# Threshold attention with a Fourier mixing block: q and k transposed by VectorE in 32x32 blocks, and one block-diagonal score product for the last 64 queries

## The chip, the core and the metric

The kernel runs on one core of a Trainium2 chip. The metric is the device time of one execution in microseconds. The engines are TensorE (PE; its weight loads are listed as PEld), VectorE (DVE), ScalarE (ACT), GpSimd (POOL) and SyncE (SP), which issues most DMAs. TensorE writes to PSUM; the other data lie in SBUF.

## The reference

Attention in 8 batches of 8 heads, 576 queries and keys, head dimension 64, all float32. A weight counts only where its score lies within tau of the row's maximum. Then a Fourier mixing over sequence and channels, and a normalised two-layer channel network with 512 and 2048 channels.

```python
scores = (1 / sqrt(64)) * q @ k.transpose(0, 1, 3, 2)      # q, k, v: (8, 8, 576, 64)
thresh = max(scores, -1) - tau
scores = where(scores >= thresh, scores, -1e9)
attn = exp(scores - max(scores)); attn = attn / (sum(attn) + 1e-9)
x = (attn @ v) with heads side by side                      # (8, 576, 512)
u = x + real(fft over channels of fft over sequence of x)
un = (u - mean(u)) / sqrt(var(u) + 1e-6)
out = u + relu(un @ w_ch1) @ w_ch2                          # float64 in memory: 512 x 2048, 2048 x 512
```

## The kernel before

The attention works on pairs of heads: 4 pairs in each of 8 batches, so 32 pairs, numbered n. A pair has 5 steps, t = 0 to 4, so there are 160 steps i = 5n + t. Steps 0 to 3 take 128 queries of each of the two heads. Step 4 takes the last 64 queries of both heads together, head j on partitions 64j to 64j+63 of one tile.

`load_pair(n)` (L124) fetches q and k of a pair with ten DMAs into `qk_in`, rows of 64 floats (256 bytes) per query or key, so that the tokens lie on the partitions. For k of the second head the blocks are placed so that its transposed columns come out rotated by 64. There is one such buffer (`bufs=1`). `prep_in_parts(n)` (L389) turns the pair round: four PE transposes into `pq` (L398), evacuated by DVE into `qT` with the factor q_scale (L399); four into `pk` (L405), evacuated by ACT into `kT` (L406); one into `pt` (L409), evacuated by DVE in two parts (L410, L413). Then it issues `load_pair(n + 1)`. In `qT` and `kT` head j lies on partitions 64j to 64j+63, the columns are tokens.

`scores(i)` (L423) multiplies: for t < 4 four products of 64 rows, two heads by two halves of 288 keys (L433); for t = 4 five products of 64 rows and 64 columns (L444), one of them cut because of the rotated columns. `softmax(i)` (L450) takes the row's maximum on DVE (L461), the exponential on ACT (L469), the threshold and sum on DVE (L477), and later scaling on DVE and ACT (L492, L496). `weights_in_parts` (L512) transposes the weights on PE (L560), `weighted_values` (L569) multiplies with v (L589). Each matmul appears as two records in the profile.

PSUM is used through two rings: "sc" with two score tiles, and "mm" with four banks that all other PE results share, the transposes among them.

Between the attention's steps lies other PE work. `mixing` does the Fourier part of the batch before, `channels` and `channels_in_quarters` do the channel network: hidden layer products (L822, L926), output products (L848, L1090). `fill()` (L1169) takes as much of it as a budget per slot allows. POOL does sums for these products (`s_w` L909, `t_u` L900, `s_tile` and `hs` L1086), and the folding of x (`half` L622, after an exchange of two rows by DMA, L607 and L609).

There are three parts. In the first batch, `step(i)` (L1185) puts all engines' instructions in order by hand and prepares the next pair at t = 4; there is no channel work yet, so `busy` issues matmuls whose result is not used, and the weights are converted from float64 on the side. In the second batch, `second_batch(i)` (L1316) is ordered by hand too and prepares at t = 3, between the second and third `fill()`. From the third batch on, the loop at L1387 fixes only the order of PE; the other engines' order is made by the framework's scheduler. There the three parts of the preparation are spread over the step t = 3. After the last attention step, what is left of the channel network runs alone.

Of the kernel before, what the change touches and what calls it, by code (L numbers as in the profile page):

```python
# [47 lines left out]
def kernel(  # L48
# [75 lines left out]
    def load_pair(n, queue=nc.sync):  # L124
        b, p = n // NPAIR, PAIRS[n % NPAIR]
        hs = [2 * p + (j + p) % 2 for j in range(2)]

        qk = sb.tile([128, 9, 2, D], FP32, tag="qk", bufs=1, name="qk_in")
        for j, h in enumerate(hs):
            nc.sync.dma_start(  # L130
                out=qk[:, 0:4, j, :], in_=q[b, h, 0:512, :].rearrange("(t p) d -> p t d", p=128)
            )
            nc.sync.dma_start(out=qk[0:64, 8, j, :], in_=q[b, h, 512:576, :])


        h = hs[0]
        queue.dma_start(
            out=qk[:, 4:8, 0, :], in_=k[b, h, 0:512, :].rearrange("(t p) d -> p t d", p=128)
        )
        queue.dma_start(out=qk[64:128, 8, 0, :], in_=k[b, h, 512:576, :])  # L140
        h = hs[1]
        queue.dma_start(out=qk[0:64, 4, 1, :], in_=k[b, h, 512:576, :])
        rows = k[b, h, 0:512, :].rearrange("(t r p) d -> p r t d", r=2, p=64)
        queue.dma_start(out=qk[64:128, 4:8, 1, :], in_=rows[:, 0])
        queue.dma_start(out=qk[0:64, 5:8, 1, :], in_=rows[:, 1, 0:3])
        queue.dma_start(out=qk[64:128, 8, 1, :], in_=rows[:, 1, 3])
        loaded[n] = qk

    def load_v(n):

# [20 lines left out]
    for u in range(2):  # L171
        for j in range(2):
            nc.gpsimd.memset(v_in[u][64 - 64 * j : 128 - 64 * j, 8 + j, :], 0.0)
    eps = const.tile([128, 1], FP32, name="eps")
    nc.vector.memset(eps[:], 1e-6)

# [205 lines left out]
    xs = {}  # L382
    sums = {}

    def prep_pair(n):
        for _ in prep_in_parts(n):
            pass

    def prep_in_parts(n):  # L389


        qk = loaded.pop(n)
        qT = sb.tile([128, S], FP32, tag="qT", name="qT")
        kT = sb.tile([128, S], FP32, tag="kT", name="kT")

        pq = ps.tile([128, 512], FP32, tag="mm", bufs=4, name="pq")
        for t in range(4):
            nc.tensor.transpose(pq[:, 128 * t : 128 * t + 128], qk[:, t, :, :], ident[:, :])  # L398
        nc.vector.tensor_scalar(  # L399
            out=qT[:, 0:512], in0=pq[:, :], scalar1=q_scale[:, :], scalar2=None, op0=ALU.mult  # L400
        )
        yield
        pk = ps.tile([128, 512], FP32, tag="mm", bufs=4, name="pk")
        for t in range(4):
            nc.tensor.transpose(pk[:, 128 * t : 128 * t + 128], qk[:, 4 + t, :, :], ident[:, :])  # L405
        nc.scalar.copy(kT[:, 0:512], pk[:, :])  # L406
        yield
        pt = ps.tile([128, 512], FP32, tag="mm", bufs=4, name="pt")
        nc.tensor.transpose(pt[:, 0:128], qk[:, 8, :, :], ident[:, :])  # L409
        nc.vector.tensor_scalar(  # L410
            out=qT[:, 512:S], in0=pt[:, 0:64], scalar1=q_scale[:, :], scalar2=None, op0=ALU.mult
        )
        nc.vector.tensor_copy(kT[:, 512:S], pt[:, 64:128])  # L413
        heads[n] = (qT, kT, v_in[n % 2])
        if n + 1 < B * NPAIR:
            load_pair(n + 1)

    def normalized(n):

# [3 lines left out]
    def scores(i):  # L423
        n, t = divmod(i, NT)
        qT, kT = heads[n][0:2]

        nh = 2 if t < 4 else 1
        sc = [ps.tile([128, 2, 512], FP32, tag="sc", name=f"sc{j}") for j in range(nh)]
        if t < 4:
            for c in range(2):  # L430
                for j in range(2):
                    hp = slice(64 * j, 64 * j + 64)
                    nc.tensor.matmul(  # L433
                        sc[j][:, c, 0:HALF], qT[hp, 128 * t : 128 * t + 128],
                        kT[hp, HALF * c : HALF * (c + 1)], start=True, stop=True,
                    )
        else:

            for j, c, c0, k0, w in (
                (0, 0, 0, 0, HALF), (1, 0, 0, 64, HALF), (0, 1, 0, HALF, HALF),  # L440
                (1, 1, 0, 64 + HALF, 512 - HALF), (1, 1, 512 - HALF, 0, 64),
            ):
                hp = slice(64 * j, 64 * j + 64)
                nc.tensor.matmul(  # L444
                    sc[0][hp, c, c0 : c0 + w], qT[hp, 512:S], kT[hp, k0 : k0 + w],
                    start=True, stop=True, skip_group_check=True,
                )
        steps[i] = (sc, nh)

# [735 lines left out]
    def step(i):  # L1185

        n, t = divmod(i, NT)
        scores(i)

        def last_stages():  # L1190
            run = chunks.pop(i - 1, None)
            for _ in range(2 if run else 0):
                next(run, None)

        if t == 1 and n > 0:
            softmax(i, lambda: weighted_values(n - 1, 1), last_stages)
            load_v(n + 1)
        elif t == 3:
            softmax(i, lambda: weighted_values(n, 0), last_stages)
        else:  # L1200
            softmax(i, None, last_stages)
        if t == 1 and n > 0:
            pass
        elif later and later[0][0] <= i:
            later.pop(0)[1](i)
        else:
            busy(2 if i < NCHUNK else 1)
        if t == NT - 1:
            prep_pair(n + 1)
        if i in chunks:  # L1210
            next(chunks[i])
        if i > 0:
            transposed_weights(i - 1)
        if i in chunks:
            next(chunks[i])
        while after and after[0][0] <= i:
            after.pop(0)[1]()
        if i > 0 and i + 3 < NCHUNK:
            chunks[i + 3] = w1_chunk(i + 3)
        if t == 2 and n > 0:  # L1220
            folds.append(fold_rows(n - 1))
        if folds and next(folds[0], True):
            folds.pop(0)
# [27 lines left out]
    raw = load_dim()  # L1251
    load_seq()
    chunks[1] = w1_chunk(1)
    prep_pair(0)
    load_v(0)
    chunks[2] = w1_chunk(2)
# [59 lines left out]
    def second_batch(i):  # L1316

        nonlocal budget
        n, t = divmod(i, NT)
        first = i - per_batch  # L1320
        if first != 1:
            scores(i)
        if first == 0:

            transposed_weights(i - 1)
        softmax(i, None, lambda: (advance(first - 1), advance(first - 1)))
        chunks.pop(first - 1, None)
        transfers(first)
        fold_more()
        if first == 0:  # L1330
            weighted_values(n - 1, 1)
            scores(i + 1)
            column_means(LAST)
            copy_mean(LAST)
            folds.append(fold_rows(n - 1))
            while folds:
                fold_more()
            load_v(n + 1)
            start_batch(0)
            mix(3)  # L1340
            mix(3)
        elif first == 1:
            mix(3)
            transposed_weights(i - 1)
            mix(2)
            mirrored(LAST)
            for c, eng in ((1, nc.vector), (3, nc.vector), (0, nc.gpsimd), (2, nc.gpsimd)):
                less_mean(eng, LAST, c)
            advance(first)
            advance(first)  # L1350
        elif first == 2:
            mix(2)
            transposed_weights(i - 1)
            mix(2)
            weighted_values(n, 0)
            advance(first)
            advance(first)
        else:
            fill()
            transposed_weights(i - 1)  # L1360
            advance(first)
            advance(first)
            fill()
            if t == 3:
                prep_pair(n + 1)
            fill()
            if t == 2:
                weighted_values(n, 0)
            if t == 0:
                weighted_values(n - 1, 1)  # L1370
                folds.append(fold_rows(n - 1))
                load_v(n + 1)
        if first == 16:
            fold_halves(1)
        if first < 3:
            budget += 3 * per_slot
# [10 lines left out]
    for i in range(2 * per_batch, total + 1):  # L1387
# [4 lines left out]
        n, t = divmod(i, NT)  # L1392
        if t > 2:
            fold_more()
        nothing = iter(())
        prep = prep_in_parts(n + 1) if t == 3 and n + 1 < B * NPAIR else nothing
        weights = weights_in_parts(i - 1)
        next(prep, None)
        fill()
        next(weights, None)  # L1400
        fill()
        next(weights, None)
        next(prep, None)
        if i < total:
            softmax(i)
        fill()
        next(prep, None)
        if t == 2:
            weighted_values(n, 0)
        if t == 0:  # L1410
# [60 lines left out]
```

## Time and profile before

| | |
|---|---|
| Time, median of 3 runs | 1670.19 us (1670.05 to 1670.26) |
| Span of the profiled execution | 1669.6 us |
| Preparations of pairs, first and last start | 9.4 us, 1409.9 us |
| First scores, last scores of t = 4 | 11.6 us, 1462.7 us |
| q1, the queue of nearly all transfers | 128854 packets, 55.35 MB |
| HBM read, written | 46.02 MB, 9.44 MB |

Times in the profile are microseconds unless marked ns. A group of instructions is given by line, engine, operation, tile written and tiles read, shape and count. A tile query gives for each line the shortest, median and longest duration in ns, then the first and last start. A list of waits gives engine and line, what was waited for, and then the total in us, the number of waits and the longest. In a list in order of time an entry has its start and its length; several equal instructions in a row are merged, and lengths of matmuls in a row overlap.

### The profile page before, as it was taken

Reading aid. Unit: us, or ns where it says so; the run is one execution under the profiler, and the core shown is the slowest. Engines: PE = TensorE matmul, PEld = TensorE weight load, DVE = VectorE, ACT = ScalarE, POOL = GpSimd, SP = SyncE. Lnnn points to the kernel's source line nnn. Section 1 sums busy time; section 2 is a strip of 40 time slices with the busy share of each in tenths; the row PEclk is TensorE's granted clock in tenths of the full one; section 3 lists DMA queues with packets and bytes.
Section 4 is the critical chain, followed back from the end, with each engine's and each line's share of the span. In section 5 each row is a group of like instructions: output and inputs, shape, how many; then the busy total and the mean of one; then the engine's idle time right before and its main releaser. Section 6 shows DMA issues by size and latency. Waiting matters only on the chain.

```text
span 1669.6 us, 28885 instructions
## 1 busy us (share of the span) xinstructions
PE 1621.8 (97%) x10826; PEld 1273.6 (76%) x10826; DVE 1146.0 (69%) x2518; ACT 837.9 (50%) x1817; POOL 581.9 (35%) x779
## 2 busy tenths in 40 slices
PE   8998899999999999999999999999999999999998
PEld 4555555577887888878888778887878788889998
DVE  6887785567757686857566858686677768664454
ACT  5775675544455454545354546454646455532111
POOL 5674562041321442134332143213242244215232
PEclk9999999999999999999999999999999999999999
DMA  5423222100010101000101010111001010000000
GB/s 157 121 55 110 73 73 56 30 20 21 19 39 15 29 15 42 23 28 8 28 22 35 10 34 15 42 22 29 22 16 42 22 32 4 14 1 13 14 13 13
DMA packets 130384, 57.48 MB, mean 34 GB/s; under 512 B 121123, under 2 KB 121125, under 8 KB 130246
## 3 DMA queue, kind: packets, MB, share of 16 engines
q1 hardware_dynamic: 128854, 55.35, 12.3%
q8 instruction: 86, 1.41, 0.4%
q14 instruction: 52, 0.43, 0.1%
q10 hardware_dynamic: 1392, 0.30, 0.1%
HBM read 46.02 MB, written 9.44 MB: 33 GB/s over the span
## 4 chain that ended last, share of the span: by engine, by line
PE 76%; DVE 15%; ACT 7%; issue 2%; POOL 1%; DVEq 0%; ACTq 0%; POOLq 0%
PE ph L926 23%; PE po L1090 18%; PE pv L589 8%; PE sc L433 7%; PE pw L560 5%; PE po L848 3%; DVE e L477 3%; DVE neg L461 2%; ACT e L469 2%; DVE hs L1051 2%; PE sc L444 2%; PE ph L822 1%; PE py L692 1%; PE pa L709 1%; PE pn L782 1%
## 5 line engine op out<-in xcount | busy, mean ns | idle before, releaser
L469 ACT ACTIVATE e<-sc,neg 128x576 f32<-128x576 f32 x288 | 212.6, 738 | 238.1 <-DVE neg L461 237.4
L461 DVE TENSOR_REDUCE neg<-sc 128x1 f32<-128x576 f32 x288 | 206.2, 750 | 171.4 <-PE sc L433 158.5
L477 DVE SCALAR_TENSOR_TENSOR e<-sc,thr,e 128x576 f32<-128x576 f32 x288 | 229.7, 811 | 57.5 <-ACT thr L473 54.2
L1090 PE MATMUL po<-w,hs 128*128 128x256 f32 x1024 | 246.3, 383 | 0.5 <-DVE u L804 0.5
L1090 PEld LDWEIGHTS po<-w,hs 128*128 128x128 f32 x1024 | 186.0, 190 | 33.6 <-issue 11.2
L926 PE MATMUL ph<-u_t,w 128*128 128x128 f32 x1536 | 187.2, 276 | 0.0
L926 PEld LDWEIGHTS ph<-u_t,w 128*128 128x128 f32 x1536 | 178.7, 192 | 4.4 <-issue 3.3
L560 PE MATMUL pw<-ident,e 128*128 128x128 f32 x1152 | 169.5, 274 | 10.4 <-ACT kT L406 2.7
L562 ACT COPY e_t<-pw 128x512 f32<-128x512 f32 x256 | 148.9, 596 | 59.8 <-PE pw L560 59.3
L433 PE MATMUL sc<-kT,qT 64*128 64x288 f32 x1024 | 168.6, 429 | 6.8 <-DVE e L477 6.0
L560 PEld LDWEIGHTS pw<-ident,e 128*128 128x128 f32 x1152 | 134.2, 141 | 29.3 <-issue 4.3
L935 DVE TENSOR_TENSOR hs<-ph,hs 128x512 f32<-128x512 f32 x160 | 106.9, 685 | 71.4 <-PE ph L926 46.8
L433 PEld LDWEIGHTS sc<-kT,qT 64*128 64x128 f32 x1024 | 93.2, 186 | 69.3 <-issue 37.2
L926 PE MATMUL ph<-t_u,s_w 128*128 128x128 f32 x1024 | 126.0, 276 | 2.2 <-POOL t_u L900 1.8
L804 DVE SCALAR_TENSOR_TENSOR u<-po,rstd,u 128x256 f32<-128x256 f32 (+1 forms) x164 | 75.4, 484 | 73.8 <-PE po L1090 71.9
L926 PEld LDWEIGHTS ph<-t_u,s_w 128*128 128x128 f32 x1024 | 119.4, 192 | 5.3 <-issue 2.6
L1090 PE MATMUL po<-hs,s_tile 128*128 128x256 f32 x512 | 122.1, 382 | 0.0
L496 ACT ACTIVATE e<-e,den 128x576 f32<-128x576 f32 x96 | 75.0, 781 | 67.4 <-DVE den L489 66.7
L1090 PEld LDWEIGHTS po<-hs,s_tile 128*128 128x128 f32 x512 | 93.6, 190 | 13.6 <-issue 2.1
L943 ACT ACTIVATE hs<-hs 128x512 f32<-128x512 f32 x112 | 69.4, 631 | 63.9 <-DVE hs L935 63.9
L622 POOL TENSOR_TENSOR half<-x 128x287 f32<-128x287 f32 x48 | 40.4, 862 | 125.5 <-ACT x L595 70.7
L1086 POOL TENSOR_TENSOR hs<-hs,s_tile 128x512 f32<-128x512 f32 x32 | 42.3, 1323 | 117.5 <-PE po L1090 113.8
(199 smaller groups left out, 2905.8 us busy)
## 6 DMA issues: line engine op xcount, KB each, us to landing
hs<-in_moe_w_ch_dram SPq DMA_DIRECT2D x23, 512.0 KB, 4.4
out_dram<-u SPq DMA_DIRECT2D x36, 256.0 KB, 2.2
qk_in<-in_q_dram SPq DMA_DIRECT2D x64, 128.0 KB, 2.3
v_in<-in_v_dram SPq DMA_DIRECT2D x64, 128.0 KB, 2.4
qk_in<-in_k_dram SPq DMA_DIRECT2D x31, 128.0 KB, 2.5
w<-in_moe_w_ch_dram SPq DMA_DIRECT2D x6, 512.0 KB, 8.4
qk_in<-in_k_dram SPq DMA_DIRECT2D x31, 64.0 KB, 2.3
stage<-in_moe_w_ch_dram SPq DMA_DIRECT2D x3, 512.0 KB, 3.8
```

What stands on the lines that cost most here:

```text
L433: nc.tensor.matmul(sc[j][:, c, 0:HALF], qT[hp, 128 * t : 128 * t + 128], kT[hp, HALF * c : HALF * (c + 1)], start=True, stop=True,)
L461: nc.vector.tensor_reduce(out=neg[:, j : j + 1], in_=sc[j][:, :, 0:HALF], axis=AXIS_XY, op=ALU.max, negate=True,)
L469: nc.scalar.activation(out=ej, in_=sc[j][:, :, 0:HALF], func=ACT.Exp, bias=neg[:, j : j + 1], scale=1.0)
L477: nc.vector.scalar_tensor_tensor(out=ej, in0=sc[j][:, :, 0:HALF], scalar=thr[:, j : j + 1], in1=ej, op0=ALU.is_ge, op1=ALU.mult, accum_out ...
L496: nc.scalar.activation(out=e[:, S : 2 * S], in_=e[:, S : 2 * S], func=ACT.Copy, scale=den[:, 1:2])
L560: nc.tensor.transpose(pw[:, c, :], e[:, c0 : c0 + 128], ident[:, :])
L562: nc.scalar.copy(e_t[:, 4 * j : 4 * j + 4, qs], pw[:, :, :])
L589: nc.tensor.matmul(pv[64 * j : 64 * j + 64, 0:m], vt[:, 2 * c + j, :], e_t[:, 4 * j + c, 0:m] if c < 4 else ends[:, 0:m], start=(c == 0), ...
L804: nc.vector.scalar_tensor_tensor(out=u, in0=product, scalar=self.rstd[:, t : t + 1], in1=u, op0=ALU.mult, op1=ALU.add,)
L926: nc.tensor.matmul(banks[name][:, 128 * q : 128 * q + 128], left[c][:, 512 * part + 128 * q : 512 * part + 128 * q + 128], right[c], start ...
L935: nc.vector.tensor_tensor(out=to, in0=bank, in1=to if other is None else other, op=ALU.add)
L1090: nc.tensor.matmul(bank[:, 0 : DM // 2], left[p], right[p], start=start and p == 0, stop=p == NK - 1, skip_group_check=True,)
```

## The change

q and k are loaded in blocks of 32 features: for each head and each half g of the 64 features one DMA brings, for r = 0 to 17, the tokens 32r to 32r+31 onto 32 partitions, 32 floats (128 bytes) each. That makes eight DMAs a pair, four for q and four for k, into `q_in` and `k_in` (128 partitions x 576). Transposing each 32x32 block in place then gives features on partitions and tokens in columns, for both heads.

`scale_q(n)` multiplies q by q_scale in place, for the first pair on ACT and otherwise on POOL. `prep_pair(n)` makes the transposes on DVE: all of k into columns 64 to 639 of `kT`, which grows by 64 columns; the second head's last 64 keys again, into columns 0 to 63 of its partitions; and all of q into `qT`, of which there is now one buffer. The first head's keys therefore lie in order from column 64, and the second head's can be read rotated from column 0, or in order from column 64.

For the last 64 queries `prep_ends(n)` copies the two heads' 64x64 blocks of qT on POOL into a 128x128 tile `q_ends` whose other blocks are zero. Two products of 128 rows and 128 columns, one for each half of the keys, give both heads' scores.

In all three parts `prep_ends(n)` comes at t = 1 and `scale_q(n + 1)` at t = 2. `prep_pair(n + 1)` stays at t = 4 in the first batch, moves from t = 3 to t = 4 in the second, and is undivided at t = 3 in the rest, ahead of the first `fill()`.

```diff
@@ load_pair
-        qk = sb.tile([128, 9, 2, D], FP32, tag="qk", bufs=1, name="qk_in")
-        for j, h in enumerate(hs):
-            nc.sync.dma_start(
-                out=qk[:, 0:4, j, :], in_=q[b, h, 0:512, :].rearrange("(t p) d -> p t d", p=128)
-            )
-            nc.sync.dma_start(out=qk[0:64, 8, j, :], in_=q[b, h, 512:576, :])
...
+        for src, name, eng in ((q, "q_in", nc.sync), (k, "k_in", queue)):
+            raw = sb.tile([128, S], FP32, tag=name, bufs=1, name=name)
+            for j, h in enumerate(hs):
+                for g in range(2):
+                    p = 64 * j + 32 * g
+                    eng.dma_start(
+                        out=raw[p : p + 32, :].rearrange("p (r d) -> p r d", d=32),
+                        in_=src[b, h, :, 32 * g : 32 * g + 32].rearrange(
+                            "(r p) d -> p r d", p=32
+                        ),
+                    )
+            raws.append(raw)
+        loaded[n] = raws
@@ constants
+    q_ends = const.tile([128, 128], FP32, name="q_ends")
+    nc.gpsimd.memset(q_ends[:, :], 0.0)
@@ in place of prep_in_parts
+    def scale_q(n):
+        raw = loaded[n][0]
+        if n == 0:
+            nc.scalar.activation(out=raw[:, :], in_=raw[:, :], func=ACT.Copy, scale=q_scale[:, :])
+        else:
+            nc.gpsimd.tensor_scalar(
+                out=raw[:, :], in0=raw[:, :], scalar1=q_scale[:, :], scalar2=None, op0=ALU.mult
+            )
     def prep_pair(n):
-        for t in range(4):
-            nc.tensor.transpose(pq[:, 128 * t : 128 * t + 128], qk[:, t, :, :], ident[:, :])
-        nc.vector.tensor_scalar(
-            out=qT[:, 0:512], in0=pq[:, :], scalar1=q_scale[:, :], scalar2=None, op0=ALU.mult
-        )
...
+        q_raw, k_raw = loaded.pop(n)
+        kT = sb.tile([128, D + S], FP32, tag="kT", name="kT")
+        nc.vector.transpose(kT[:, D : D + S], k_raw[:, :])
+        nc.vector.transpose(kT[64:128, 0:D], k_raw[64:128, 512:S])
+        qT = sb.tile([128, S], FP32, tag="qT", bufs=1, name="qT")
+        nc.vector.transpose(qT[:, :], q_raw[:, :])
         heads[n] = (qT, kT, v_in[n % 2])
         if n + 1 < B * NPAIR:
             load_pair(n + 1)
+
+    def prep_ends(n):
+        for j in range(2):
+            hp = slice(64 * j, 64 * j + 64)
+            nc.gpsimd.tensor_copy(q_ends[hp, hp], heads[n][0][hp, 512:S])
@@ scores
-                    hp = slice(64 * j, 64 * j + 64)
+                    hp, k0 = slice(64 * j, 64 * j + 64), D * (1 - j)
...
-                        kT[hp, HALF * c : HALF * (c + 1)], start=True, stop=True,
+                        kT[hp, k0 + HALF * c : k0 + HALF * (c + 1)], start=True, stop=True,
...
-            for j, c, c0, k0, w in (
-                (0, 0, 0, 0, HALF), (1, 0, 0, 64, HALF), (0, 1, 0, HALF, HALF),
-                (1, 1, 0, 64 + HALF, 512 - HALF), (1, 1, 512 - HALF, 0, 64),
-            ):
-                hp = slice(64 * j, 64 * j + 64)
+            for c in range(2):
                 nc.tensor.matmul(
-                    sc[0][hp, c, c0 : c0 + w], qT[hp, 512:S], kT[hp, k0 : k0 + w],
-                    start=True, stop=True, skip_group_check=True,
+                    sc[0][:, c, 0:HALF], q_ends[:, :], kT[:, D + HALF * c : D + HALF * (c + 1)],
+                    start=True, stop=True,
                 )
@@ second_batch
+        if t == 1:
+            prep_ends(n)
+        if t == 2:
+            scale_q(n + 1)
...
-            if t == 3:
+            if t == 4:
                 prep_pair(n + 1)
@@ loop from the third batch on
-        prep = prep_in_parts(n + 1) if t == 3 and n + 1 < B * NPAIR else nothing
...
+        if t == 1:
+            prep_ends(n)
+        if t == 2 and n + 1 < B * NPAIR:
+            scale_q(n + 1)
+        if t == 3 and n + 1 < B * NPAIR:
+            prep_pair(n + 1)
```

More of the change, by code (lines that the diff above doesn't have):

```diff
@@ L126, in load_pair @@
         hs = [2 * p + (j + p) % 2 for j in range(2)]
-        qk = sb.tile([128, 9, 2, D], FP32, tag="qk", bufs=1, name="qk_in")
-        for j, h in enumerate(hs):
-            nc.sync.dma_start(
-                out=qk[:, 0:4, j, :], in_=q[b, h, 0:512, :].rearrange("(t p) d -> p t d", p=128)
-            )
-            nc.sync.dma_start(out=qk[0:64, 8, j, :], in_=q[b, h, 512:576, :])
-        h = hs[0]
-        queue.dma_start(
-            out=qk[:, 4:8, 0, :], in_=k[b, h, 0:512, :].rearrange("(t p) d -> p t d", p=128)
-        )
[L140 to L147, printed above, removed]
+        raws = []
+        for src, name, eng in ((q, "q_in", nc.sync), (k, "k_in", queue)):
[11 more added lines that the diff above has]
+        loaded[n] = raws
     def load_v(n):
@@ L383 @@
     sums = {}
-    def prep_pair(n):
[L386 to L396, printed above, removed]
-        for t in range(4):
-            nc.tensor.transpose(pq[:, 128 * t : 128 * t + 128], qk[:, t, :, :], ident[:, :])
-        nc.vector.tensor_scalar(
-            out=qT[:, 0:512], in0=pq[:, :], scalar1=q_scale[:, :], scalar2=None, op0=ALU.mult
[L401 to L413, printed above, removed]
+    def scale_q(n):
[6 more added lines that the diff above has]
+            )
+    def prep_pair(n):
+        q_raw, k_raw = loaded.pop(n)
[4 more added lines that the diff above has]
+        nc.vector.transpose(qT[:, :], q_raw[:, :])
         heads[n] = (qT, kT, v_in[n % 2])
@@ L1253 @@
     chunks[1] = w1_chunk(1)
+    scale_q(0)
     prep_pair(0)
@@ L1329, in second_batch @@
         fold_more()
+        if t == 1:
+            prep_ends(n)
+        if t == 2:
+            scale_q(n + 1)
         if first == 0:
@@ L1394 @@
             fold_more()
-        nothing = iter(())
-        prep = prep_in_parts(n + 1) if t == 3 and n + 1 < B * NPAIR else nothing
         weights = weights_in_parts(i - 1)
-        next(prep, None)
+        if t == 1:
+            prep_ends(n)
+        if t == 2 and n + 1 < B * NPAIR:
+            scale_q(n + 1)
+        if t == 3 and n + 1 < B * NPAIR:
+            prep_pair(n + 1)
         fill()
@@ L1402 @@
         next(weights, None)
-        next(prep, None)
         if i < total:
@@ L1406 @@
         fill()
-        next(prep, None)
         if t == 2:
```

## The prediction

> **What bounds the kernel now.** I read the page first: busy shares, then the clock by slice.
>
> ```profile
> PE 1621.8 (97%) x10826; PEld 1273.6 (76%) x10826; DVE 1146.0 (69%) x2518; ACT 837.9 (50%) x1817; POOL 581.9 (35%) x779
> PEclk9999999999999999999999999999999999999999
> ```
>
> TensorE is the candidate, but matmul ends are modelled, so a busy share alone proves little. Second, busy time by stretch; the columns are the stretch, its length, busy us and instructions of PE, PEld, DVE, ACT, POOL, then clock and DMA.
>
> ```profile
> 281.00:374.00 93.00, 92.01 (x523) 57.35 (x523) 54.22 (x137) 46.25 (x106) 19.35 (x31) 1.00 0.11 29
> 374.00:1476.00 1102.00, 1086.26 (x7707) 892.65 (x7704) 778.84 (x1717) 571.92 (x1215) 334.15 (x442) 1.00 0.09 24
> ```
>
> From 281 to 1476 us PE is idle only 17 us of 1195, at full clock, while DVE is 70% and POOL 30% busy. (Before 281, fifty-microsecond stretches have PE at 44 to 49 of 50; after 1476 no attention is left.) Third, what PE waits for in that stretch:
>
> ```profile
> PE py L692 <- ACT ends L548: 3.1, 2, 1.6
> PE pv L589 <- ACT e_t L562: 2.4, 3, 0.8
> PE pw L560 <- DVE qT L399: 1.9, 4, 0.5
> PE ph L926 <- POOL t_u L900: 1.8, 1, 1.8
> ```
>
> No wait is large, so there time is PE work, and work taken from PE is time. Fourth, PE in order of time around one preparation (start, length, operation), to see how long the removed work holds the queue:
>
> ```profile
> 1181.11 0.66 PE L398 MATMUL pq<-ident,qk_in 128*128 128x128 f32 x4
> 1181.60 1.95 PE L926 MATMUL ph<-t_u,s_w 128*128 128x128 f32 x16
> ...
> 1186.15 0.60 PE L405 MATMUL pk<-ident,qk_in 128*128 128x128 f32 x4
> 1186.59 1.95 PE L926 MATMUL ph<-u_t,w 128*128 128x128 f32 x16
> 1188.38 0.27 PE L409 MATMUL pt<-ident,qk_in 128*128 128x128 f32 x1
> 1188.58 1.20 PE L444 MATMUL sc<-kT,qT 64*64 64x288 f32 x10
> 1189.70 0.49 PE L926 MATMUL ph<-u_t,s_w 128*128 128x128 f32 x2
> ```
>
> The reader should see that one transpose has 273 ns as its duration but the next instruction starts about 110 ns later. The differences of starts count: 0.49 (pq), 0.44 (pk), 0.20 (pt), 1.12 (last queries' scores). Pricing nine transposes at 273 ns would say 2.46 us a pair, twice too much.
>
> Last, the evacuations that leave with them:
>
> ```profile
> L399 DVE TENSOR_SCALAR qT<-pq,q_scale x32: 731/741/751, 10.5 to 1412.0; 128x512 f32<-128x512 f32 x32
> L410 DVE TENSOR_SCALAR qT<-pt,q_scale x32: 251/274/284, 11.2 to 1420.1; 128x64 f32<-128x64 f32 x32
> L413 DVE COPY kT<-pt x32: 206/211/219, 11.3 to 1420.3; 128x64 f32<-128x64 f32 x32
> L406 ACT COPY kT<-pk x32: 558/592/687, 10.9 to 1416.1; 128x512 f32<-128x512 f32 x32
> ```
>
> [...] the eight half-height score records of one tile (L433), 403 ns each, take 1.18 us from start to next start, not 3.2. [...]
>
> **The change, part by part.**
>
> PE, removed: nine transposes a pair. Over the 24 preparations from 281 us on, the starts give 0.54 + 0.44 + 0.20 = 1.18 us a pair on average (leaving out one idle of 0.54), 28.3 us in all. This lies on the bounding engine.
>
> PE, last 64 queries: ten records in 1.12 us become four (two products of 288 columns, two records each, as elsewhere). A record of 256 columns takes 216 ns in long runs (2.59 us for 12, L1090), so 288 take 243, four 0.97[...]. Gain 0.13 by 25 tiles from 281 us on = 3.3 us. Bounds 0.0 to 0.2 each.
>
> DVE: removed 0.741 + 0.274 + 0.211 = 1.23 us a pair. Added: two transposes of 576 columns and one of 64. No row shows this; the nearest, the 576-column reduction (L461), takes 0.75. [...] Sum 1.8, net +0.6 us a pair. [...] I take +0.6. At 70% DVE load behind a busy PE most is hidden; the transposes come two steps (some 18 us) ahead of the first scores that read them in the late loop.
>
> ACT loses 0.59 us a pair; the "mm" PSUM ring loses three tenants a pair. ACT is at 52% and PE waits little on either, so I count nothing.
>
> POOL, added: scaling q in place (128x576) and two 64x64 copies into q_ends. A POOL copy of 128x630 (L536) takes 0.71 and a two-input 128x512 operation (L1086) 1.3, so 0.7 to 1.5; with the copies 1.1 to 2.1, middle 1.6 us a pair. POOL is at 30%. scale_q (t=2) is a step, some 9 us, ahead of the late transposes, prep_ends (t=1) three steps ahead of its reader; hidden unless POOL is stuck. Behind scale_q on POOL wait s_w, s_tile and fold operations, which PE needs later.
>
> SP: ten q/k issues (370 to 630 ns) become eight with 576 runs of 128 bytes each: 4608 packets instead of 2304. In 900-946 us, 3680 packets took 8.6% of 16 engines, 17 ns each; at the same price per packet, 4608 take 4.9 us spread over 16 engines, at double 9.8. Issue at t=3 to use at t=2 is some 37 us, so nothing. SP waits for the DVE transposes where it waited for pt, about 1 us later; v loads, swaps and stores behind it have slack.
>
> First batch (to about 130 us, by hand, one step of notice). At 38 us PE transposes run while the softmax chain is on DVE; the next scores started at 41.48. Without them DVE goes on after its reciprocal (ends 40.02) with 1.8 us of transposes (slightly overlapped, 1.7): scores at about 41.8. Four boundaries by +0.3 = +1.2; with the dear transposes +1.5 each, +6. At the very start scores waited until 11.56 for transposed data; now four k transfers instead of six on ACT's queue, and six busy matmuls that end at 10.0: -1.0 (bounds -1.5 to +2).
>
> Second batch before 281 us (three pairs): PE loses 3 x 1.3 = 3.9 of work at 90 to 98% load, while preparation moves from t=3 to t=4, one fill before its reader, behind softmax and weight conversion on DVE. Bounds -3.9 to +4; I take -1.5.
>
> Late stalls from more DVE and POOL work: 0.1 us by 24 pairs = +2.5 (bounds 0 to 10).
>
> Sum: -28.3 - 3.3 + 1.2 - 1.0 - 1.5 + 2.5 = -30.4. Made against the span of 1669.6; the timed runs have median 1670.19 (1670.05 to 1670.26), 0.6 more, so 1670.2 - 30.4 = **1640**.
>
> **Rivals.**
> 1. Forecast, 1640; own range 1630 to 1651. For it: PE idle of 1.4% and no large wait.
> 2. DVE takes over part of it: transposes at half rate. +6 instead of +1.2 at the start, +3 instead of -1.5 in the second batch, late stalls +10: -28.3 - 3.3 + 6 - 1 + 3 + 10 = -13.6, **1657**. [...] Against: DVE's slack of 30%.
> 3. Slower: POOL holds DVE, DVE holds PE. scale_q stands in POOL's in-order queue behind an operation waiting for PE (s_w waits for PE's ph 14 times, 133.9 us, 9.6 each); the qT transpose waits in front of DVE's evacuations, and PE runs out of its four PSUM banks after about four products of 1.8 us (16 records of 112 ns), 7.2 us. It decides from a stall above 1.3 us a pair. At 9.6 - 7.2 = 2.4 us by 24 pairs, +58: 1670 - 30 + 58 = **1698**. For it: the waits exist. Against: scale_q depends on nothing but an early load, and a whole step lies between.
> 4. Late transfers, so that the gain is eaten: would need 4608 packets to last over 30 us, 104 ns each against 17. About **1670**.
>
> **How the numbers follow.** Chances: forecast 0.60, rival 2 0.20, rival 3 0.12, rival 4 or gains that cancel 0.04, a larger gain (freed PSUM banks and ACT time also remove waits, 1625) 0.04. A measurement here tells 0.2%, 3.3 us, from no change. Faster: 0.60 + 0.20 + 0.04 = 0.84; same 0.03; slower 0.13. The range takes in the forecast's bounds and rival 2: 1628 to 1660.
>
> **What would show it.** Right: PE busy down by some 75 us as printed (32 x 9 transposes at 273 ns), but the stretch of PE at 98% shorter by 30; L444 with four records in about 1.0 us; DVE transposes of 0.7 to 0.8; scores after the first boundary near 41.8. Wrong: DVE transposes above 1.2 us, PE waiting for DVE's kT, qT or evacuations more than 0.5 us a pair, or DVE idle before qT with POOL's scaling as releaser. A PE share below 96% between 281 us and the end of attention would refute "PE work is time".

## The result, and the profile after

| | before | after |
|---|---|---|
| Time, median | 1670.21 us (1670.05 to 1670.26) | 1659.59 us (1657.76 to 1662.54) |
| Span of the profiled execution | 1669.6 us | 1655.7 us |
| Ratio after to before | | 0.9938, 95% interval 0.9921 to 0.9955 |

The change makes the kernel faster by 10.6 us, 0.6%, where 30 us were forecast. The direction held, and the time lies within the stated range. The amount did not come: it is a third of the forecast. The two profiled executions lie further apart, 13.9 us by their spans: the one before took 1671.4 us, above its median, and the one after 1657.8, the fastest of its four. What the traces show below accounts for the 13.9.

The page of the changed kernel, the busy shares and then the clock by slice:

```profile
PE 1584.1 (96%) x10346; PEld 1248.7 (75%) x10346; DVE 1170.7 (71%) x2518; ACT 820.9 (50%) x1786; POOL 660.1 (40%) x875
PEclk9999989999999999999999999999999999999999
```

PE has 480 records fewer, 15 a pair: nine transposes, which are one record each here and not two, and four score records instead of ten. Its printed busy time is 38 us less. DVE rose by 25 us and POOL by 78. The clock shows a lower slice early on that the kernel before did not have.

The groups that are new, with count, then busy us and mean ns, then idle before:

```profile
L390 POOL TENSOR_SCALAR q_in<-q_in,q_scale 128x576 f32<-128x576 f32 x31 | 56.7, 1828 | 21.1 <-DMA q_in<-in_q_dram 19.8
L404 DVE STREAM_TRANSPOSE qT<-q_in 128x576 f32<-128x576 f32 x32 | 24.7, 770 | 0.3
L401 DVE STREAM_TRANSPOSE kT<-k_in 128x576 f32<-128x576 f32 x32 | 24.6, 769 | 3.4 <-DMA k_in<-in_k_dram 3.4
L402 DVE STREAM_TRANSPOSE kT<-k_in 64x64 f32<-64x64 f32 x32 | 7.7, 242 | 0.6
```

The DVE transposes take 770 and 242 ns, 1.78 us a pair where the forecast took 1.8; that 1.8 was the author's estimate, and no trace had shown such a transpose. So rival 2, transposes at half rate, is out: above 1.2 us was named as the sign against the forecast. That its 1657 us is the number nearest to the measured 1659.6 is chance. POOL's scaling takes 1.83 us on average, above the bound of 1.5.

Where the time went is seen from the start of each pair's first scores in the two traces (PE in order of time). The last column is after minus before.

| first scores of pair | before, us | after, us | difference |
|---|---|---|---|
| 0 | 11.56 | 9.89 | -1.67 |
| 4 (second batch begins) | 132.22 | 132.27 | +0.05 |
| 5 | 178.59 | 185.94 | +7.35 |
| 6 | 215.84 | 230.66 | +14.82 |
| 8 (third batch begins) | 288.40 | 305.04 | +16.64 |
| 9 | 340.27 | 354.78 | +14.51 |
| 31 | 1426.18 | 1412.49 | -13.69 |

From pair 9 to pair 31 the change gains 28.2 us, 1.28 a pair, close to the forecast (1.31 less a little for stalls). The second batch alone loses 16.6 us. There PE waits, as a list of PE's waits for the whole execution shows. The first scores of a pair waited for the preparation in the kernel before too, but for 0.6 us in all:

```profile
PE sc L430 <- DVE qT L404: 27.7, 8, 8.5
PE sc L430 <- DVE e L469: 7.2, 14, 1.4
PE ph L814 <- POOL u_t L727: 3.6, 1, 3.6
```

The longest of these waits, in order of time (the changed kernel, from the last scores of pair 5 to the first of pair 6):

```profile
217.38 1.14 PE L436 MATMUL sc<-kT,q_ends 128*128 128x288 f32 x4
...
220.74 0.75 DVE L453 TENSOR_REDUCE neg<-sc 128x1 f32<-128x576 f32 x1
...
223.99 0.82 DVE L469 SCALAR_TENSOR_TENSOR e<-sc,thr,e 128x576 f32<-128x576 f32 x1 [1.30 <-ACT thr L465]
...
225.57 1.11 DVE L297 TENSOR_SCALAR w<-stage 128x512 int32<-128x512 int32 x1
...
226.47 1.35 POOL L319 TENSOR_TENSOR w<-w,w 128x512 f32<-128x512 f32 x1
...
226.60 1.50 DVE L300 TENSOR_SCALAR u_t<-stage 128x512 int32<-128x512 int32 x1
...
228.03 0.51 DVE L297 TENSOR_SCALAR w<-hs 128x512 int32<-128x512 int32 x1
...
228.45 0.41 DVE L300 TENSOR_SCALAR hs<-hs 128x512 int32<-128x512 int32 x1
...
228.79 0.77 DVE L401 STREAM_TRANSPOSE kT<-k_in 128x576 f32<-128x576 f32 x1
...
229.82 0.78 DVE L404 STREAM_TRANSPOSE qT<-q_in 128x576 f32<-128x576 f32 x1
...
230.66 1.81 PE L430 MATMUL sc<-kT,qT 64*128 64x288 f32 x6 [8.47 <-DVE qT L404]
```

Read it from below. PE has had nothing to do for 8.47 us. The transposes themselves are 1.8 us of that. In front of them, in DVE's queue, stand the maximum of step 4, its threshold, which waits 1.30 us for ACT, and then the conversion of w_ch2 for two chunks (L297, L300).

One thing in this queue is longer than its work. L300 takes 1.50 us for the first chunk and 0.41 for the second. When the first starts, POOL's L319 is running, and it ends 0.28 us after that (228.10 against 227.82). Another one-input DVE line, the later scaling of the weights, shows the same many times over:

```profile
L484 DVE TENSOR_SCALAR e<-e,den x120: 477/520/1566, 310.1 to 1455.3; 128x576 f32<-128x576 f32 x120
```

It takes 0.48 to 0.52 us in the 71 cases in which POOL does nothing. Of the 33 cases over 0.6 us, 32 end 0.31 to 0.32 us after the end of a POOL operation that ran beside them. So in these cases DVE is held until POOL is done; in the other 16 cases beside a POOL operation L484 takes 0.51 to 0.54 us. In the list above the hold makes L297 (1.11 against 0.51 us for the second chunk) and L300 together some 1.7 us longer, of the 11.4 from the last scores to the transposes. The large transposes don't show it: all 64 take 0.76 to 0.78 us, and POOL works beside 33 of them.

The same stretches of both kernels by window (stretch, length, busy us and instructions of PE, PEld, DVE, ACT, POOL, clock, DMA). Before:

```profile
130.00:310.00 180.00, 164.47 (x889) 99.51 (x890) 134.62 (x317) 110.67 (x257) 78.27 (x98) 0.99 0.26 75
310.00:1450.00 1140.00, 1124.59 (x7878) 912.37 (x7877) 795.09 (x1760) 586.46 (x1251) 349.14 (x468) 1.00 0.10 24
```

After:

```profile
130.00:310.00 180.00, 149.18 (x748) 90.11 (x748) 127.23 (x282) 101.18 (x237) 89.68 (x113) 0.92 0.27 72
310.00:1450.00 1140.00, 1125.07 (x7719) 913.10 (x7718) 832.35 (x1818) 589.84 (x1264) 408.96 (x539) 1.00 0.12 25
```

After 310 us PE is as full as before (1125 of 1140 us): there less PE work is less time. Between 130 and 310 us PE is busy 15 us less in the same stretch, and its clock is 0.92 instead of 0.99.

### The profile page after: what moved, and what is told of

The parts are those of the page before. It is cut to its first block, busy times and chain, and to the rows that moved or that the text cites. A ratio compares the mean times of both kernels' runs of the same rounds, so it can differ in the third digit from the quotient of the medians.

```text
span 1655.7 us, 27993 instructions
## 1 busy us (share of the span) xinstructions
PE 1584.1 (96%) x10346; PEld 1248.7 (75%) x10346; DVE 1170.7 (71%) x2518; ACT 820.9 (50%) x1786; POOL 660.1 (40%) x875
## 3 DMA queue, kind: packets, MB, share of 16 engines
q1 hardware_dynamic: 200438, 55.34, 14.2%
## 4 chain that ended last, share of the span: by engine, by line
PE 77%; DVE 14%; ACT 5%; issue 2%; POOL 1%; DVEq 0%; ACTq 0%; POOLq 0%
PE ph L918 23%; PE po L1082 20%; PE pv L581 9%; PE sc L430 8%; PE pw L552 5%; PE po L840 3%; DVE e L469 3%; DVE neg L453 2%; PE ph L814 2%; ACT e L461 2%; PE sc L436 1%; PE py L684 1%; PE pn L774 1%; PE pa L701 1%; DVE hs L1043 1%
## 5 line engine op out<-in xcount | busy, mean ns | idle before, releaser
L461 ACT ACTIVATE e<-sc,neg 128x576 f32<-128x576 f32 x288 | 212.2, 737 | 229.1 <-DVE neg L453 228.7
L469 DVE SCALAR_TENSOR_TENSOR e<-sc,thr,e 128x576 f32<-128x576 f32 x288 | 229.5, 813 | 50.5 <-ACT thr L465 49.0
L430 PE MATMUL sc<-kT,qT 64*128 64x288 f32 x1024 | 169.3, 434 | 35.0 <-DVE qT L404 27.7
```

The costliest lines, as they stand in the source:

```text
L430: nc.tensor.matmul(sc[j][:, c, 0:HALF], qT[hp, 128 * t : 128 * t + 128], kT[hp, k0 + HALF * c : k0 + HALF * (c + 1)], start=True, stop=True,)
L461: nc.scalar.activation(out=ej, in_=sc[j][:, :, 0:HALF], func=ACT.Exp, bias=neg[:, j : j + 1], scale=1.0)
L469: nc.vector.scalar_tensor_tensor(out=ej, in0=sc[j][:, :, 0:HALF], scalar=thr[:, j : j + 1], in1=ej, op0=ALU.is_ge, op1=ALU.mult, accum_out ...
```

## The experiments

The theory (A): the loss is the place of the preparation in the second batch, t = 4 behind softmax and weight conversion. The rivals: the DVE transposes or the narrow transfers themselves are too dear there (B), or the lower clock that follows a wait (0.69 between 230 and 240 us, behind the 8.47 us above).

**Back to t = 3 in the second batch, transposes kept.**

```diff
-            if t == 4:
+            if t == 3:
                 prep_pair(n + 1)
```

> The changed kernel, with the second batch's preparation back at t = 3 (VectorE transposes kept). Theory A, the place: at t = 4 the transposes stand on DVE behind the last 64 queries' softmax and the weight conversion, with one fill of PE work to cover them, and PE waits at four boundaries of pairs (9.9, 14.8, 15.0, 16.6 us lost against before by the first scores of pairs 5 to 8, 15 to 17 in sum); then 14 to 17 us come back: 1643 to 1646 us. Theory B, the DVE transposes or the narrow transfers are themselves too dear in this stage, where DVE also converts weights: 1656 to 1662 us, with the waits only at another step.

Measured: 1645.76 us (1644.76 to 1649.2), ratio 0.9864 (0.9846 to 0.9882). 13.8 us came back. PE's waits for qT between 130 and 310 us, from the list of waits of the changed kernel:

```profile
PE sc L430 <- DVE qT L404: 20.3, 5, 8.5
```

And from that of this kernel, in the same stretch:

```profile
PE sc L430 <- DVE qT L404: 3.5, 2, 3.0
```

The transposes run one step earlier at the same price, so B does not hold. Of the 3.5 us that are left, 3.0 belong to the boundary from pair 3 to pair 4, which the first batch prepares. Not all of the stage is won back: from the first scores of pair 4 to those of pair 8 this trace still takes 3.0 us longer than the kernel before, where a gain was forecast.

**The kernel before, with only that move.** The same edit in the other direction, in the kernel with PE transposes.

> The kernel before (PE transposes, 256-byte rows), with only the second batch's preparation moved from t = 3 to t = 4. Theory A, the place alone costs: PE's own transposes are out early but their DVE and ACT evacuations stand in the same place, so the first scores of pairs 5 to 8 wait too: 1678 to 1687 us. Theory B, it is the DVE transposes and not the place: 1668 to 1673 us.

Measured: 1682.77 us (1680.15 to 1683.89), ratio 1.0078 (1.0063 to 1.0093): the move alone costs 12.7 us. Between 130 and 310 us PE now waits at the same place, for the last evacuation instead of the last transpose. Here that one is on ACT, behind ACT's own part of the conversion:

```profile
PE sc L433 <- ACT kT L406: 8.8, 3, 4.9
```

The first scores come 11.1 us late at pair 8 and the lag then stays (12.4 at pair 31). So the loss does not need the DVE transposes: the move alone makes it.

**t = 4 kept, but ahead of that step's softmax.** PE's order is unchanged; the three transposes stand some ten instructions earlier in DVE's queue. The loads of the next pair, which `prep_pair` issues, move forward with them; but between 130 and 310 us no transpose waits for a transfer in either version.

```diff
+        if t == 4:
+            prep_pair(n + 1)
         softmax(i, None, lambda: (advance(first - 1), advance(first - 1)))
...
-            if t == 4:
-                prep_pair(n + 1)
```

> The changed kernel, with the second batch's preparation still at t = 4 but issued ahead of that step's softmax instead of behind it, the weight conversion and a fill. PE's order is the same. Theory A1, it is the place in DVE's queue: the waits of the first scores of pairs 5 to 8 shrink to under 1 us and most of the 15 us comes back: 1644 to 1650 us. Theory A2, it is the step: any place at t = 4 is too late for first scores one step on: 1655 to 1662 us.

Measured: 1646.32 us (1645.64 to 1647.2), ratio 0.9862 (0.9847 to 0.9877), as good as t = 3. In order of time at the same boundary as above:

```profile
219.27 0.76 DVE L401 STREAM_TRANSPOSE kT<-k_in 128x576 f32<-128x576 f32 x1
220.05 0.24 DVE L402 STREAM_TRANSPOSE kT<-k_in 64x64 f32<-64x64 f32 x1
220.32 0.78 DVE L404 STREAM_TRANSPOSE qT<-q_in 128x576 f32<-128x576 f32 x1
221.02 0.72 DVE L453 TENSOR_REDUCE neg<-sc 128x1 f32<-128x576 f32 x1
...
221.87 0.75 PE L430 MATMUL sc<-kT,qT 64*128 64x288 f32 x2
```

The first scores start at 221.87 instead of 230.66. Of these 8.8 us, 3.2 were there already at pair 5, where the same wait is gone too. It is the place in DVE's queue, not the step.

**PE kept at work during the wait.** Four products whose result is not used after the last `fill()` of t = 4.

```diff
             fill()
+            if t == 4:
+                busy(4)
```

> The changed kernel, with four more unused 128x512 products after the last fill at t = 4 in the second batch, where PE waits for qT (some 3.4 us at full clock, where it idles 3 to 8.5). If a good part of the 15 us is the lower PE clock that follows each wait (0.69 to 0.83 in the ten microseconds after), the time falls by 2 to 6 us: 1653 to 1657. If the wait alone is the loss, 1658 to 1662, or more where the products outlast the wait.

Measured: 1659.60 us (1657.22 to 1661.08), the time of the changed kernel. PE's clock between 130 and 310 us rose from 0.92 to 0.96 and the waits for qT there fell from 20.3 to 3.0 us, since the products fill them, and nothing was gained. The wait is the loss; a cost of the clock beside it does not show in the sum. It is not excluded: where the products last longer than the wait, they cost what a higher clock may bring.

**The first batch at t = 3 too.**

```diff
-        if t == NT - 1:
+        if t == NT - 2:
             prep_pair(n + 1)
```

> As e1_second_at_3, and the first batch's preparation at t = 3 too. Theory A: the first batch's boundaries also wait for qT (three waits, 7.4 us, in the first 135 us of the changed kernel), so 3 to 7 us more come back than in e1: 1637 to 1642 us. Rival: in the first batch DVE is over 80% busy and itself the bound, so the 1.8 us of transposes cost the same wherever they stand: within 2 us of e1.

Measured: 1640.34 us (1639.02 to 1642.01), ratio 0.9826 (0.9812 to 0.9841), and in a second set of runs 1639.69 us (1637.69 to 1641.33), ratio 0.9822 (0.9809 to 0.9836). It beats both kernels. That it meets the forecast of 1640 is chance: it gains in the first batch, which was not forecast, and not in the second, which was. The first scores of pair 1 start at 36.72 us, against 39.41 after and 41.48 before.

**Both at t = 3, the second batch ahead of the softmax.** As the one before, with `prep_pair` moved as in the experiment on DVE's queue.

> As e3_first_and_second_at_3, with the second batch's preparation at t = 3 ahead of the softmax. Theory A (what decides is that the transposes are done before PE comes to the next pair): nothing left to gain by going further ahead, 1638 to 1643 us. Rival: every DVE operation ahead of a softmax delays that step's weights; slower than e3 by more than 3 us.

Measured: 1642.04 us (1639.36 to 1644.1), ratio 0.9834 (0.982 to 0.9847), within the theory's span and not told apart from the version behind the softmax.

**The DVE transposes doubled in the late loop.**

```diff
+        for _ in range(2 if late else 1):
             nc.vector.transpose(kT[:, D : D + S], k_raw[:, :])
             nc.vector.transpose(kT[64:128, 0:D], k_raw[64:128, 512:S])
...
             nc.vector.transpose(qT[:, :], q_raw[:, :])
```

> The changed kernel, with the three DVE transposes done twice in every preparation of the loop from the third batch on (23 preparations, the second writes the same values). Theory: DVE has room there and PE is the bound, so 23 x 1.78 = 41 us of DVE work cost under 3 us: 1658 to 1664 us. Rival, DVE is the hidden bound there and takes over: half of it or more shows, over 1680 us.

Measured: 1664.12 us (1659.74 to 1664.4), ratio 0.9961 (0.9947 to 0.9974). The transposes' busy time rises from 57.0 to 97.7 us. From the first scores of pair 9 to those of pair 31 it takes 1060.5 us against 1057.7: 2.8 us for 22 preparations, 39 us of DVE work. Other versions with the same late loop as the changed kernel take 1056.2 to 1057.8 us for this stretch. In the late loop DVE has room; the time is at the upper edge of what was expected.

**The block-diagonal product taken back.** Four products of 64 rows and 64 columns from the same tiles.

```diff
-                nc.tensor.matmul(
-                    sc[0][:, c, 0:HALF], q_ends[:, :], kT[:, D + HALF * c : D + HALF * (c + 1)],
-                    start=True, stop=True,
-                )
+                for j in range(2):
+                    hp = slice(64 * j, 64 * j + 64)
+                    nc.tensor.matmul(
+                        sc[0][hp, c, 0:HALF], q_ends[hp, hp],
+                        kT[hp, D + HALF * c : D + HALF * (c + 1)],
+                        start=True, stop=True, skip_group_check=True,
+                    )
```

> The changed kernel, with the last 64 queries' scores as four products of 64 rows and 64 columns (two heads by two halves, each head's own block of q_ends) in place of two of 128 rows and 128 columns. Theory: in the changed kernel the two take 0.97 us from start to next start against 1.12 before, so the block-diagonal form is worth 0.15 us a pair where PE is the bound: the stretch from the first scores of pair 9 to those of pair 31 (1057.7 us) becomes 22 x 0.15 = 3.3 us longer, the time 1661 to 1665 us. Rival: its worth is nothing, since two of the four run side by side: same stretch within 1 us, 1657 to 1662 us.

Measured: 1668.08 us (1663.62 to 1670.64), ratio 0.9987 (0.9981 to 0.9994). The stretch from pair 9 to pair 31 takes 1064.9 us, 7.2 more, 0.33 a pair: twice what was expected. PE in order of time shows where it is. The changed kernel:

```profile
1402.67 2.76 PE L1082 MATMUL po<-hs,s_tile 128*128 128x256 f32 x12
1405.26 1.14 PE L436 MATMUL sc<-kT,q_ends 128*128 128x288 f32 x4
1406.23 1.03 PE L1082 MATMUL po<-hs,s_tile 128*128 128x256 f32 x4
1407.09 1.03 PE L1082 MATMUL po<-w,hs 128*128 128x256 f32 x4
```

With four products:

```profile
1411.12 2.76 PE L1085 MATMUL po<-hs,s_tile 128*128 128x256 f32 x12
1413.80 1.19 PE L438 MATMUL sc<-kT,q_ends 64*64 64x288 f32 x8
1414.92 1.13 PE L1085 MATMUL po<-hs,s_tile 128*128 128x256 f32 x4
1415.89 1.03 PE L1085 MATMUL po<-w,hs 128*128 128x256 f32 x4
```

From start to next start: 2.59, 0.97, 0.86 against 2.68, 1.12, 0.97. The scores cost 0.15 more, as expected, but the same twelve products ahead cost 0.09 more and the four behind 0.11. After 340 us all 24 places show the 0.09 ahead, and 22 of them some 0.10 behind: sixteen products of the hidden layer, for instance, take 1.88 ahead of the four score products against 1.79 ahead of the two, and 1.89 against 1.78 behind them. So each side of a 64x64 group between 128x128 work shows about 0.1 us; what takes it, no run isolates.

**Scaling of q at t = 1 in the second batch.** The version with both preparations at t = 3, with one more move. In all versions with DVE transposes pair 4 still took 50 us or more instead of 46 in the first traces, and there scale_q stands on POOL ahead of additions into u_t that PE's first channel product needs.

```diff
         if t == 1:
             prep_ends(n)
-        if t == 2:
             scale_q(n + 1)
```

> As e3_first_and_second_at_3, with scale_q(n + 1) at t = 1 instead of t = 2 in the second batch, nothing else moved. In pair 4, at t = 2, the 1.9 us of scaling stand on POOL ahead of six additions into u_t that PE's next channel product waits for (3.4 us against 1.7 before), and the PE clock is at 0.5 in the five microseconds after. Theory: this is the 4 us that pair 4 still takes longer in e1, e3 and e6; moved to where POOL is idle, the wait falls to 1.7 us or less, pair 4 takes 46 to 48 us instead of 50.5, and the time is 2 to 4 us below e3 on the same chip. Rival: those 4 us come from elsewhere, time within 1 us of e3.

The version to compare with, on the same chip:

> e3_first_and_second_at_3 once more, beside e10_scale_at_1 on the same chip: 1638 to 1643 us; pair 4 takes 50.5 us from its first scores to those of pair 5.

Measured: 1640.12 us (1639.81 to 1641.01), ratio 0.9827 (0.9813 to 0.984), against 1639.69 for the other. PE's wait is shorter. In the list of waits of the version with scale_q at t = 2 (second set) it is

```profile
PE ph L814 <- POOL u_t L727: 3.4, 1, 3.4
```

and in that of the version with it at t = 1

```profile
PE ph L814 <- POOL u_t L727: 2.1, 1, 2.1
```

Nothing of it is left in the time: by pair 6 the two are within 1 us of each other. The expectation was wrong on the other version as well: in its second trace pair 4 takes 47.7 us, not 50.5, with the same wait, while PE's clock stays at 1.00; in its first trace the clock fell to 0.50 between 165 and 170 us. So some 3 of those 4 us came and went between two traces of one program, together with the clock; that the clock is their cause is not shown.

## Why the prediction was right or wrong

- **What bounds the kernel: right.** From pair 9 to 31 the gain is 28.2 us by 22 pairs. Doubling the DVE transposes there costs 2.8 us, so the time is PE's. By the traces, the start gained 1.7 us (1.0 forecast), the first batch lost 1.7 (1.2), and from pair 8 on the kernel gained 30.5 (29.1). These terms together are off by under 2 us, and the second batch by 18.
- **The step that failed** is "Second batch before 281 us (three pairs) ... Bounds -3.9 to +4; I take -1.5." By the first scores of pair 8 the changed kernel had lost 16.6 us there. I had seen the move from t = 3 to t = 4 and named what is ahead of the transposes ("behind softmax and weight conversion on DVE"), but gave the queue in front of them no price: at pair 6 it is 11.4 us from the start of the last scores to the start of the transposes. Moving just the transposes forward in that queue gave 13.3 us back, moving them a step earlier 13.8; the kernel before loses 12.7 by that move alone. The sign that was named for being wrong did show: PE waits for qT 27.7 us, 0.87 a pair against the 0.5 that was named, all of it by the start of pair 8. The move is a separate edit and costs more than half of the 24.4 us that the rest gains (1670.2 less 1645.8). The term was also too good without the move: the 3.9 us of PE work saved there were to be a gain, yet with the preparation at t = 3 the traces lose 0.1 to 7.4 us from pair 4 to pair 8. Why is open.
- **PE, removed: the sum right, its two parts off.** Transposes were priced at 1.18 us a pair and the ends at 0.13 (1.12 less 0.97 is 0.15; the 0.02 taken off was the author's allowance). What pq takes above the 0.44 of pk (0.49 to 0.62), and pt above 0.11, was counted as price of the transposes. The runs point to the neighbours with another tile size: sixteen products of the hidden layer (128x128) right behind scores of 64 rows take 1.89 us, and 1.79 behind others. Part of that stays, since other products now stand beside those scores, and part belongs to the last queries' scores. Nine transposes are then about 0.99 us (an estimate from pk's 0.44 for four), and the ends 0.33, as measured by taking them back. That the sum is 1.32 against 1.31 is chance: two errors of 0.2 us cancel.
- **Signs on PE: one mis-sized.** Printed busy time was to fall by 75 us and fell by 38. The forecast added the full lengths of records that overlap, and the page counts an overlap once. For the same reason 1.18 us for eight records is not to be held against 3.2, as the forecast did, but against twice the 0.97 that four records of 128 rows and 128 columns take; it is below that too.
- **DVE: right**, 1.78 us a pair against 1.8. Rows of the trace before come to the same (an estimate: two of 0.75, the 576-column reduction L461, and one of 0.21 to 0.27, the 64-column L413 and L410, make 1.7 to 1.8). Less the 1.23 that left, this makes 18 us; the printed rise is 25, and the rest lies in other DVE operations. Late stalls: 2.5 us were counted, the late stretch shows about 0.6 (1.31 x 22 = 28.8, less 28.2).
- **POOL: size off.** 1.83 for the scaling and two copies of 0.32, 2.5 us a pair, above the bound of 2.1. Hidden nearly everywhere, as said; at one place in pair 4 a wait of PE for POOL is twice as long (3.6 us against 1.7), and shortening it to 2.1 left no trace in the time.
- **SP and transfers: right.** A q or k transfer lands in 2.3 to 2.4 us (median), 2.2 to 2.7 before. The main queue carries 71,584 packets more for 14.2% instead of 12.3% of 16 engines: about 476 us, some 7 ns for each packet more (an estimate from rounded shares), under the 17 assumed.
- **First batch and start: right in sum.** The first boundary, put at about 41.8 us, came at 39.4, earlier than by the start alone; the loss is at the second and the fourth. Moved to t = 3, the first boundary gains 1.1 to 3.3 us, which was not looked for; by pair 4 one of the four traces has lost that again.
- **Rival 3**, slower through POOL and DVE, named the right form (PE waiting for DVE) in the wrong place and for another reason: mainly DVE's own queue in the hand-ordered batch, where POOL's hold on DVE is a part, and not POOL's scaling in the scheduled loop.

What stays open: what the second batch still loses with its preparation at t = 3; the lower clock of PE in the first 310 us, which differs between traces of one program; and how much of the spread of the times it explains (1657.8 to 1662.5 us for the changed kernel; 1667.7 to 1671.7 for the kernel before beside the experiments).

## What to carry to other kernels

Price a moved step by everything that stands ahead of it in the queue of the engine that runs it, from the trace, until the reader needs it; the step's own length says little. Take time differences from starts, not from printed durations, and look at the neighbours of a group with another tile size, since they can pay too (here about 0.1 us on each side of a 64x64 group). Where a DVE operation is longer in one place than in another, look at what POOL does beside it (here up to 1.57 us against 0.52). When a change of several edits brings less than its sum, compare the starts of one recurring instruction in both traces: here one table showed the stage, and a single edit brought 14 us back.

## What the runs showed of the hardware

- A DVE transpose of 128x576 float32 in 32x32 blocks takes 0.77 us, 64x64 takes 0.24 (changed kernel, 64 and 32 of them).
- A group of four 64x64 products between 128x128 products cost about 0.1 us more on each side than two products of 128 rows and 128 columns in its place (0.09 us ahead at 24 of 24 places, some 0.10 behind at 22).
- A one-input DVE operation (128x576 float32, L484, 0.52 us alone) took up to 1.57 us beside a POOL operation, and ended 0.31 to 0.32 us after it in 32 of 33 long cases; in 16 more cases beside one it took 0.51 to 0.54. DVE transposes of 128x576 stayed at 0.76 to 0.78 us, 33 of 64 beside a POOL operation.
- POOL takes 1.73 us (median) to scale 128x576 float32 by a per-partition factor, while it copies 128x630 in 0.71: here one input did not make an operation cheap.
- PE's granted clock was 0.50 between 165 and 170 us in one trace of a program (both preparations at t = 3) and 1.00 in another of the same; between 130 and 310 us it was 0.92 in the changed kernel and 0.99 in the kernel before.
